# One core, gated linear attention and a tanh-shrink MLP: three sums planned apart, a load moved, a copy moved to another engine, and a new order of work

## The chip, the core and the metric

One core of one Trainium2 chip runs the whole program. The metric is device microseconds of one execution, from timed runs; beside them one execution was recorded by the profiler, and every duration below that is not a time of a run comes from that record. The engines are PE (matmuls, with weight loads shown apart as PEld), DVE and ACT (element-wise work), POOL (set-up only here) and SP (issues transfers). Each engine works through its own queue in order.

## The reference

```python
for t in range(S):                                   # q, k, v, alpha: (4, 8, 768, 48) fp32
    state = alpha[:, :, t, :, None] * state + einsum('bhd,bhe->bhde', k[:, :, t], v[:, :, t])
    y[:, :, t] = einsum('bhd,bhde->bhe', q[:, :, t], state)
x = y.transpose(0, 2, 1, 3).reshape(3072, 384)       # (B*S, H*D)
h = x @ w_in                                         # (384, 2048)
out = (h - tanh(h)) @ w_out                          # (2048, 384)
```

A recurrence over 768 tokens for 4 x 8 heads, and behind it two matrix products with h - tanh(h) between them.

## The kernel before, in words

**Units and steps.** The 3072 tokens are cut into 12 units of 256 tokens (u = 0 to 11), each of two chunks of 128 (c = 0, 1). For each unit an attention part makes `xT`, the transposed features, and an MLP part takes them through 8 steps (s = 0 to 7) of 256 hidden features each.

**The attention part.** alpha, k and q are loaded and transposed (units 0 and 1 by PE, `turn aT`, `turn kT`, `turn qT`, with alpha's results copied to SBUF by ACT and DVE, `aTa` and `aTb`; later units by DVE). DVE scans alpha's products from the end (`U`) and, scaled by the reciprocal of a chunk's whole product (`ends`), from the start (`W`); then k is multiplied by U (`kU`) and q by W (`qW`). PE transposes k back (`back`), ACT copies it (`natural`), PE forms k times v (`update`, which needs v) and the scores; DVE masks them (`masked`); PE forms the rows `y`. ACT (`x`) and DVE copy the results to `xT`; the copy named `rest` takes the last rows of 64 tokens each. For units 2 and later one PE task, the `scores` visit, forms the scores of one chunk and `y` of the chunk before in one PSUM bank pair, so the next visit waits for both copies of the one before. `moves` on SP spreads the last head pair over the tiles of `xT` by transfers, and the MLP part of the unit begins with `mix` on DVE, which reads what `moves` wrote.

**The MLP part.** Units 0 and 1 are plain matmuls (`first`, `second`). Unit 2 and later use seven products in place of eight for `second`; units 3 and later (9 units, 72 steps) do so for `first` too. In those, PE makes four products (`first_a`, L1298) in one PSUM buffer; ACT copies the first (`keep`, L1303); DVE makes three dependent sums (`partial`, L1305 to L1309): the second reads what the first wrote, the third reads both. PE makes the other products (`first`, L1314 and L1316), and DVE joins both (`join`, L1321). ACT then runs three activations (`bend`, `turn`, `square`), DVE multiplies (`shrunk`) and makes five differences (`sums`), and PE multiplies by the output weights (`second`). The buffers of `first_a` and `first` are two that rotate; `partial` frees the one, `join` the other.

**The weights** come in 16 pieces (`fetch in0` to `in7`, `out0` to `out7`) as 64-bit floats. ACT makes two passes over each (`read_a`, `read`), DVE one (`bits`) and then joins both results to the 32-bit weight (a task by the piece's own name, `in0`).

**What sets the order.** All of this is entered as tasks in a planner: a name, an engine, a planned duration, a list of tasks it comes after, and a function that emits its instructions. The order in which they are emitted, over all engines, is a written list of steps through the task list, `STEPS`; the planned durations serve in finding such a list, and in the kernel they only set how many filler matmuls (`spin`, L1479) are put into PE's planned gaps before `y 0.0`. A task that appears in one piece is emitted in one piece: `partial` is one task with three instructions, and nothing of DVE's can come between them.

**Lines the prediction touches.** `load` (L613 to L637): alpha, k, q and v of a unit in two transfers each; for unit 0 the second half is issued by ACT's queue, the first by SP's. In `go("load ...")` the list of what a load comes after. `rest` (L1040): for units 2 and later one DVE copy, L1046. `partial` (L1305). Before the change SP's queue begins: aT 0, v 0, kT 0, qT 0, fetch in0, aT 1, fetch in1, in2, in3, kT 1, qT 1, fetch out0, in4, v 1 (the names stand for loads: aT for alpha, kT for k, qT for q).

Of the kernel before, what the change touches and what calls it, by code (L numbers as in the profile page):

```python
# [17 lines left out]
P = 128  # L18
HP = 64
# [309 lines left out]
class Planner:  # L329
# [6 lines left out]
        "138 3 -2 3 -2 8 -3 17 -11 -151 143 11 -10 8 -6 12 -5 12 15 -14 -11 -8 20 -11 4 -155 163 -19 -148 149 26 -15 -2 10 -167 169 -168 160 7 -160 162 5 7 "  # L336
        "-180 160 9 -16 33 -184 2 166 -167 8 172 -178 695 -529 18 512 -694 2 -1 182 -16 3 530 -5 -527 16 4 -185 168 525 -511 -176 692 -694 167 523 -503 508 "
        "-515 511 -693 170 11 -172 689 4 -530 -171 174 524 -694 -2 182 -179 1 160 541 -535 530 -517 -178 6 690 -528 -166 2 682 11 -694 8 687 3 -522 -174 697 "
        "-693 -2 700 -525 -2 512 -509 -167 173 -181 179 516 -693 11 163 -172 2 690 -691 680 -503 -2 520 -693 2 174 -6 -166 694 -687 683 -523 -168 2 11 -9 170 "
        "-168 686 -11 -676 688 -682 685 -689 2 9 157 527 -5 -521 -166 167 -163 -2 686 -682 -1 673 11 -680 -2 6 -3 1 687 -5 -681 665 -659 676 -10 11 4 -3 4 -532 "  # L340
        "-152 685 5 -692 688 -679 -8 6 -2 -2 695 -543 521 -520 -150 671 16 -685 149 1 536 -682 687 -4 -12 -478 -46 537 4 -538 539 -541 -150 151 544 -3 -691 152 "
        "39 -37 -152 698 -547 12 -6 536 -539 4 -3 539 -17 -524 523 -512 -43 35 4 30 494 11 -526 25 505 -3 -503 -34 6 535 -527 -12 529 -522 -2 539 -531 -12 5 "
        "534 -510 9 -23 514 -521 536 -507 -2 510 -5 6 -513 -20 -4 25 513 -504 506 -33 -500 -2 30 -27 -7 30 -4 505 -500 -21 55 -36 10 501 1 -509 510 -17 -513 -4 "
        "32 26 478 -533 36 -34 32 487 -463 -60 26 35 473 -506 39 -27 -8 34 -39 510 -504 8 -12 5 24 471 9 -503 2 502 -719 720 -501 3 499 -720 252 -1 471 -484 "
        "-54 1 37 1 -222 185 529 8 -499 500 -482 1 482 -477 479 -1 -499 2 18 -6 8 -5 477 -496 25 34 -27 -27 55 -27 472 -499 -3 37 -263 735 -6 -468 26 443 -506 "
        "507 -479 474 -469 29 446 4 -735 736 1 -446 451 -483 479 -732 733 -13 6 -440 -40 -2 499 -481 475 -490 487 4 -461 462 -488 7 482 4 -17 -732 750 -486 -7 "
        "494 2 3 -4 -6 -449 -37 36 -34 501 -762 756 -751 -4 756 -18 -737 761 -10 5 6 -758 740 13 6 -758 753 7 -503 502 2 2 -488 -54 -1 40 20 11 -30 -3 -36 525 "
        "-463 480 -485 486 -480 -7 488 -480 -285 769 -489 486 -765 292 26 -28 462 -751 292 476 1 11 -10 -471 -38 510 -6 7 -488 -21 518 -484 21 -59 62 474 -533 "
        "520 -460 -26 463 24 13 -536 537 -796 292 -29 520 -11 -445 -63 62 -33 504 -796 783 -782 -10 773 20 13 -12 -492 493 12 10 -21 12 -514 537 -13 -506 497 "
        "10 -38 51 -21 -1 23 -36 23 -38 -475 476 51 -823 810 -37 38 -37 61 -834 823 -527 478 61 -24 -810 836 -552 527 24 -522 510 -11 -27 -489 503 -13 38 13 "  # L350
        "-50 1 37 2 20 -21 36 -570 556 -10 -38 49 14 -24 -38 63 -536 474 1 37 -27 63 -549 514 -840 296 531 49 -35 -840 876 -64 -811 297 -40 65 490 -514 18 497 "
        "34 -526 -10 -53 62 -5 499 34 14 -603 36 554 -535 536 -523 549 -13 -12 -534 536 -530 503 26 12 -37 -501 30 -355 827 -525 -2 576 -12 -11 -497 -355 891 "
        "-27 -37 -826 296 541 -538 576 16 -594 579 -549 567 -2 -15 -13 -507 536 -55 41 -551 511 1 -482 494 -527 39 531 10 -542 515 -25 53 -41 31 -42 54 -582 "
        "571 10 -572 20 -26 526 -523 577 -11 22 -919 879 -14 -536 591 -11 24 -35 -32 68 -13 -11 -43 1 43 24 -55 -511 -69 612 -31 32 -581 550 1 -515 554 -592 "
        "554 -883 885 50 -601 550 -883 921 -36 -551 588 13 11 -23 -37 50 -39 52 -2 -612 -4 593 -26 50 -11 -38 26 13 -38 -564 604 10 -38 39 -25 26 8 -607 3 -57 "
        "1 601 -544 604 -623 575 40 9 1 -962 300 61 577 -937 337 636 -611 600 -50 62 -632 571 -547 597 -49 61 -11 12 -975 938 26 2 -15 35 -620 610 -52 63 -627 "
        "565 52 29 -80 52 -51 52 9 1 -24 -610 584 -577 -361 989 17 -610 -41 584 12 56 -17 -50 -545 614 -1 -1007 332 658 -25 -964 939 51 28 -654 628 -15 -27 69 "
        "-11 -57 -548 575 -26 -548 549 -587 643 -44 -567 635 -13 -10 -613 -32 601 25 20 -44 -572 573 -601 667 -698 699 -661 -2 -371 978 14 -659 646 32 9 -1019 "
        "366 -33 2 73 -407 336 697 -627 -38 651 -653 654 -42 66 -23 13 -55 -642 30 678 -23 -31 44 12 -1 -22 -1 13 -666 689 -67 56 12 -23 -44 68 -67 -617 -4 665 "
        "-43 67 -66 -622 623 52 -51 -623 -3 691 -64 51 -40 54 9 -48 26 -658 -55 701 -28 63 -62 41 -714 70 604 -673 735 -61 51 11 -672 -403 1051 14 -663 685 "  # L360
        "-678 -408 1075 -51 63 -711 30 670 -51 -1024 1087 -11 -51 74 -706 684 -669 618 53 -703 675 -614 651 12 -36 37 -64 52 -51 81 -80 51 12 -11 -692 693 -697 "
        "645 -588 -79 747 -669 627 -1077 1051 51 -50 12 56 -17 -50 1 67 -1120 1121 -729 711 -12 -1090 1103 -710 738 -26 16 -689 631 14 55 -10 -58 -658 717 -58 "
        "1 58 9 -757 2 21 692 -658 4 667 -26 -642 -29 727 -760 -373 1105 -27 -700 35 721 -55 66 -769 759 -756 701 -673 739 -772 762 12 -738 737 -705 -31 726 "
        "-46 -650 -33 684 47 20 -35 -1123 1092 -684 685 66 -1158 1104 43 -735 693 54 -53 1 41 -12 24 -37 -15 41 -40 41 22 -62 51 -748 760 -62 51 13 -1 -760 698 "
        "51 -12 35 -1185 409 714 63 -62 39 12 -1174 1124 -709 710 61 -22 -751 723 -1135 1162 12 -25 26 23 -34 -735 -54 761 -760 823 -784 761 10 14 -823 36 724 "
        "-721 771 25 -779 755 -756 706 75 -74 -699 749 25 -13 -1200 1176 13 -756 -15 -417 419 781 -10 -757 -432 1175 -704 729 12 17 -28 1 -759 704 -733 31 703 "
        "1 -734 735 -714 -17 811 -42 -712 686 -716 29 688 68 -1230 1212 -49 1 -723 11 723 56 12 -809 779 -24 -13 68 -42 12 18 -1231 1244 -829 799 -38 1 55 -16 "
        "-27 -741 767 18 24 -55 32 11 -809 822 -23 24 -789 720 -745 1 745 69 -14 -29 -25 55 -44 45 -12 -32 45 -810 832 -791 781 -814 758 67 -66 45 -33 55 13 "
        "-24 -12 -771 -30 851 -13 -24 -44 -777 10 836 -68 -749 -18 -3 851 -37 -43 -767 820 28 -80 1 -768 769 51 -790 740 64 -63 -754 -54 819 -751 766 63 -858 "
        "819 -11 -27 39 -789 751 39 12 -50 40 -14 -25 12 -795 833 -810 848 -846 809 -873 874 -39 -778 -56 69 766 24 -23 -781 792 49 -35 49 -62 49 -48 1 -814 "  # L370
        "826 49 -28 -840 831 -817 841 -14 -9 10 -22 66 -43 -22 1 22 -825 814 13 10 31 -42 12 44 -877 864 -867 837 -24 55 13 -846 803 -24 -820 821 67 -34 -814 "
        "792 13 30 -20 -842 843 -23 -782 825 -893 874 -843 36 808 -12 31 12 -877 -31 878 1 -818 -27 819 -816 872 -12 -43 -816 882 -856 846 -55 -850 30 886 13 "
        "-23 -13 -32 56 13 -23 -45 -864 60 860 -43 34 -908 930 -68 -828 829 -868 898 50 -874 838 -837 805 43 26 -68 -846 889 -42 1 42 -887 3 843 42 10 14 -908 "
        "843 1 -846 911 -14 -10 11 -895 844 52 13 -12 -52 65 -54 43 20 -901 -54 907 -14 -894 922 -27 62 -9 -52 -894 956 -61 52 -883 905 -36 -26 -870 898 35 13 "
        "-12 -63 76 -926 851 76 -75 47 -894 885 -886 859 37 -36 81 -44 13 -12 -11 12 -38 -885 966 -41 10 -908 859 50 -917 879 -897 936 -13 56 -42 -920 949 -41 "
        "-27 82 -81 68 -67 81 -70 1 26 -941 950 -927 -15 25 883 35 -34 25 29 -19 -920 921 -919 895 25 18 25 -41 -1 -25 -894 962 -25 12 14 -25 1 -18 -26 1 54 14 "
        "-24 11 -950 951 -45 46 12 -57 -900 -2 903 66 -20 -14 49 -14 -974 964 -56 -911 978 -10 -45 46 -14 -31 -920 921 67 -66 -955 1022 -66 -921 922 1 1 49 "
        "-1010 3 959 -957 1020 -1024 5 1005 -23 -14 38 -970 959 12 -977 939 39 -971 993 -10 -50 40 -14 -25 -938 950 48 -10 -37 -949 997 -47 1 23 13 23 -1005 "
# [69 lines left out]
def fast(tc, q, k, v, alpha, moe_w_in, moe_w_out, out, w_in, w_out, ident, ok, pad_rows):  # L448
    nc = tc.nc
    B, H, S, D = q.shape  # L450
    NP = H // 2
# [7 lines left out]
    FS = FT // 2  # L459
# [8 lines left out]
    with ExitStack() as ctx:  # L468
# [94 lines left out]
        add = plan.add  # L563
# [1029 lines left out]
```

## Time and profile before

| what | value |
|---|---|
| timed runs | 558.57, 558.87, 559.6 us; median 558.87 |
| profiled execution | 563.36 us |
| its span, first to last instruction | 561.6 us |
| mean granted clock of PE | 0.989 |
| instructions | 15127 |
| PE in 0 to 14.0 us | 10.50 of 14.00 us busy, filler included |
| last matmul ends | near 555.6 us |
| last DVE sum ends | 556.4 us |

The profiled execution is 4.5 us longer than the median of the timed runs; 1.8 us of its time lie around its span. In groups of instructions the columns are line, engine, operation, output and inputs by tile name, shapes, count, then busy time in us, mean ns of one, and the idle time of the engine just before them with what ended it. In the timeline the columns are start, length, engine, line, operation, tiles, and in brackets idle time before. Matmuls overlap each other, so a mean of 326 ns is not the distance from one start to the next.

### The profile page before, as it was taken

To read this page: it belongs to the slowest core of one execution; us is meant where nothing else is said; L and a number is where in the kernel's file an instruction comes from. 1 tells how busy PE (TensorE), PEld (TensorE's weight loads), DVE (VectorE), ACT (ScalarE), POOL (GpSimd) and SP (SyncE) were. 2 spreads that over 40 slices of the span, in tenths; PEclk is the share of its full clock that TensorE was granted. 3 is DMA by queue.
4 is the path that set the end of the run, shared out by engine and by line. 5 is a ranking of instruction groups with operands and counts; after the bars stand their busy time and mean duration, and the time that the engine had idled before them with its cause. 6 is when DMAs were issued, how large, how long until landed. Compare 5 with 4: busy or idle time off the path is not lost. (4 is left out here: it accounts for less than half of the span.)

```text
span 561.6 us, 15127 instructions
## 1 busy us (share of the span) xinstructions
PE 547.5 (97%) x6191; PEld 501.3 (89%) x6191; DVE 484.8 (86%) x1032; ACT 393.2 (70%) x746; POOL 4.9 (1%) x23
## 2 busy tenths in 40 slices
PE   7989999999999999998999999999999999999995
PEld 6877777777999999998999999999999999999995
DVE  7578659999989899999899999999999976796773
ACT  2589898967868768978668876757955654566460
POOL 3000000000000000000000000000000000000000
PEclk9699999999999999999999999999999999999999
DMA  9988482225264473535164251123020000100001
GB/s 219 240 202 245 169 204 84 88 65 146 52 135 101 114 128 107 115 117 140 35 121 113 85 157 50 48 48 85 15 51 1 30 2 8 36 2 1 30 2 33
DMA packets 60236, 50.90 MB, mean 91 GB/s; under 512 B 35552, under 2 KB 49920, under 8 KB 60160
## 3 DMA queue, kind: packets, MB, share of 16 engines
q1 hardware_dynamic: 57536, 49.07, 34.3%
q8 instruction: 51, 0.84, 0.6%
q10 hardware_dynamic: 2624, 0.79, 0.6%
q14 instruction: 25, 0.20, 0.1%
HBM read 44.04 MB, written 4.72 MB: 87 GB/s over the span
## 5 line engine op out<-in xcount | busy, mean ns | idle before, releaser
L1383 PE MATMUL o<-b,e 128*128 128x192 f32 x480 | 94.0, 326 | 0.0
L1326 ACT ACTIVATE z<-w 128x512 f32<-128x512 f32 x72 | 45.1, 626 | 54.8 <-DVE w L1321 54.7
L1383 PEld LDWEIGHTS o<-b,e 128*128 128x128 f32 x480 | 80.1, 190 | 0.8
L1383 PE MATMUL o<-w_out,e 128*128 128x192 f32 x320 | 78.6, 327 | 0.0
L1316 PE MATMUL h<-xT,w_in 128*128 128x256 f32 x288 | 74.1, 380 | 0.0
L1383 PE MATMUL o<-b,g 128*128 128x192 f32 x320 | 69.9, 326 | 0.0
L1285 PE MATMUL h<-xT,w_in 128*128 128x256 f32 (+1 forms) x300 | 66.2, 374 | 2.0 <-DVE g L1338 1.7
L1285 PEld LDWEIGHTS h<-xT,w_in 128*128 128x128 f32 x300 | 54.4, 190 | 10.9 <-DVE g L1338 1.8
L1329 ACT ACTIVATE z<-z 128x512 f32<-128x512 f32 x96 | 60.5, 630 | 1.8
L1334 ACT ACTIVATE u<-z 128x512 f32<-128x512 f32 x96 | 60.4, 629 | 1.9
L1321 DVE TENSOR_TENSOR w<-h,u 128x512 f32<-128x512 f32 x72 | 49.0, 681 | 11.8 <-PE h L1316 11.1
L1383 PEld LDWEIGHTS o<-w_out,e 128*128 128x128 f32 x320 | 55.7, 190 | 1.5
L1298 PE MATMUL h<-xT,w_in 128*128 128x128 f32 x288 | 56.4, 278 | 0.6 <-DVE w L1321 0.5
L1298 PE MATMUL h<-xT,w_out 128*128 128x128 f32 x288 | 55.8, 275 | 0.3 <-DVE xT L1245 0.3
L1383 PEld LDWEIGHTS o<-b,g 128*128 128x128 f32 x320 | 54.1, 190 | 0.4
L1316 PEld LDWEIGHTS h<-xT,w_in 128*128 128x128 f32 x288 | 49.2, 191 | 3.7
L1338 DVE TENSOR_TENSOR g<-w,u 128x512 f32<-128x512 f32 x72 | 48.8, 680 | 3.9 <-ACT u L1334 3.6
L1343 ACT ACTIVATE big<-u 128x1024 f32<-128x1024 f32 x48 | 50.7, 1055 | 0.9
L1298 PEld LDWEIGHTS h<-xT,w_in 128*128 128x128 f32 x288 | 46.7, 191 | 2.4 <-DVE w L1321 0.8
L1350 DVE TENSOR_TENSOR e<-g 128x384 f32<-128x384 f32 x80 | 43.8, 548 | 3.8 <-PE o L1383 3.3
L1303 ACT COPY u<-h 128x128 f32<-128x128 f32 x72 | 18.8, 262 | 38.2 <-PE h L1298 32.2
L1298 PEld LDWEIGHTS h<-xT,w_out 128*128 128x128 f32 x288 | 43.7, 192 | 0.5 <-DVE xT L1245 0.5
(177 smaller groups left out, 1134.9 us busy)
## 6 DMA issues: line engine op xcount, KB each, us to landing
raw<-in_moe_w_out_dram SPq DMA_DIRECT2D x16, 768.0 KB, 4.9
raw<-in_moe_w_in_dram SPq DMA_DIRECT2D x48, 96.0 KB, 4.4
raw<-in_moe_w_in_dram SPq DMA_DIRECT2D x16, 288.0 KB, 5.2
vt<-in_v_dram SPq DMA_DIRECT2D x23, 192.0 KB, 3.9
ar<-in_alpha_dram SPq DMA_DIRECT2D x20, 192.0 KB, 3.2
kr<-in_k_dram SPq DMA_DIRECT2D x20, 192.0 KB, 3.3
qr<-in_q_dram SPq DMA_DIRECT2D x20, 192.0 KB, 3.0
raw<-in_moe_w_in_dram SPq DMA_DIRECT2D x16, 192.0 KB, 4.3
```

The costliest lines, as they stand in the source:

```text
L1285: T.matmul(h[:, a, to], lhsT=w_in[:, j, f * P:(f + 1) * P], rhs=xT[u][:, j, to], start=(j == 0), stop=(j == KT - 1))
L1298: T.matmul(h[:, i], lhsT=left[n][:, s], rhs=right[u][n], start=i == 0, stop=True, skip_group_check=True)
L1303: A.copy(m["kept", s][:, 0], m["part", s][:, 0])
L1316: T.matmul(h[:, 2 * a:2 * a + 2].rearrange("p i t -> p (i t)"), lhsT=wi[:, KT - 1, s, a], rhs=xT[u][:, KT - 1, :], start=False, stop=True, ...
L1321: V.tensor_add(m["w", s], m["h", s].rearrange("p i t -> p (i t)"), m["u", s])
L1326: A.activation(m["z", s], m["h", s], AF.Tanh, scale=TA / W_SCALE)
L1329: A.activation(m["z", s], m["z", s], AF.Arctan, scale=TB)
L1334: A.activation(m["u", s], m["z", s], AF.Square, scale=TK * W_SCALE ** -0.5)
L1338: V.tensor_mul(g.rearrange("p a c t -> p (a c t)"), m["h", s], m["u", s])
L1343: A.activation(big, m["us", s // 2].rearrange("p s t -> p (s t)"), AF.Relu, bias=-F_FAST, scale=W_SCALE, accum_out=over[:, n:n + 1])
L1350: V.tensor_sub(e[:, 0:3, :], x[:, 3:4].to_broadcast([P, 3, P]), x[:, 0:3])
L1383: T.matmul(o[n][:, i], lhsT=g_, rhs=w_, start=(s_ == 0 and (n, i) in ((0, 0), (1, 0), (2, 1), (3, 0))), stop=(s_ == FS - 1), skip_group_ch ...
```

## The change

Three edits to the tasks, one to planned durations, and a new list of steps.

1. `partial` becomes three tasks, `partial_a`, `partial_b` and `partial`, with one sum each. Each comes after the one before; `join` and the PSUM buffer wait for the last, as before.
2. `load v 0` comes after `load kT 0` and `load qT 0`; a weight fetch that comes first in the list has `load aT 1` ahead of it.
3. From unit 4 on, the copy `rest` is ACT's (16 tasks).
4. Planned durations of the weight pieces, of `keep`, `join` and `rest` are changed.

```diff
-            add(f"fetch {what}{s}", "SP", ..., [held and f"read {held[0]}{held[1]}", held and f"bits {held[0]}{held[1]}"],
+            add(f"fetch {what}{s}", "SP", ..., [held and f"read {held[0]}{held[1]}", held and f"bits {held[0]}{held[1]}", n == 0 and "load aT 1"],
...
-            add(f"read_a {what}{s}", "ACT", 1.05, rank, there, lambda do=do: do(0))
-            add(f"read {what}{s}", "ACT", 1.05, rank, [f"read_a {what}{s}"], lambda do=do: do(1))
-            add(f"bits {what}{s}", "DVE", 0.6, rank, there, lambda do=do: do(2))
-            add(f"{what}{s}", "DVE", 1.0, rank, [f"read {what}{s}", f"bits {what}{s}"], lambda do=do: do(3))
+            add(f"read_a {what}{s}", "ACT", 0.96, rank, there, lambda do=do: do(0))
+            add(f"read {what}{s}", "ACT", 0.96, rank, [f"read_a {what}{s}"], lambda do=do: do(1))
+            add(f"bits {what}{s}", "DVE", 0.5, rank, there, lambda do=do: do(2))
+            add(f"{what}{s}", "DVE", 0.9, rank, [f"read {what}{s}", f"bits {what}{s}"], lambda do=do: do(3))
...
-                   + [u == 1 and ("kUb 0" if what == 3 else "turn qT 0")]
+                   + [u == 1 and ("kUb 0" if what == 3 else "turn qT 0")] + [u == 0 and what == 3 and x for x in ("load kT 0", "load qT 0")]
...
-                        V.tensor_copy(to, m["y", c].rearrange("p r g t -> p r (g t)")[0:ROWS, :, NP * (HP + D):])
+                        (A.copy if u >= 4 else V.tensor_copy)(to, m["y", c].rearrange("p r g t -> p r (g t)")[0:ROWS, :, NP * (HP + D):])
...
-                    go_c("rest", "DVE", 0.26, 10.5, [y, f"first {u - 2}:{FS - 1}"], rest)
+                    go_c("rest", "ACT" if u >= 4 else "DVE", 0.27, 10.5, [y, f"first {u - 2}:{FS - 1}"], rest)
...
-                def partial():
+                def partial(n):
                     kept, part = m["kept", s], m["part", s]
-                    V.tensor_add(kept[:, 1], kept[:, 0], part[:, 1])
-                    V.tensor_add(kept[:, 2], kept[:, 1], part[:, 2])
-                    V.tensor_add(kept[:, 1::2], kept[:, 1:3], part[:, 3:4].to_broadcast([P, 2, P]))
+                    if n < 2:
+                        V.tensor_add(kept[:, n + 1], kept[:, n], part[:, n + 1])
+                    else:
+                        V.tensor_add(kept[:, 1::2], kept[:, 1:3], part[:, 3:4].to_broadcast([P, 2, P]))
...
-                    add(f"keep {me}", "ACT", 0.26, r + 0.1, [f"first_a {me}"] + old_u, keep)
-                    add(f"partial {me}", "DVE", 0.75, r + 0.2, [f"keep {me}"], partial)
+                    add(f"keep {me}", "ACT", 0.2, r + 0.1, [f"first_a {me}"] + old_u, keep)
+                    add(f"partial_a {me}", "DVE", 0.2, r + 0.2, [f"keep {me}"], lambda: partial(0))
+                    add(f"partial_b {me}", "DVE", 0.2, r + 0.21, [f"partial_a {me}"], lambda: partial(1))
+                    add(f"partial {me}", "DVE", 0.34, r + 0.22, [f"partial_b {me}"], lambda: partial(2))
```

The list of steps is wholly new, with 2116 tasks where there were 1972. Read out by names, the queues begin as follows.

| queue | before | after |
|---|---|---|
| SP | aT 0, v 0, kT 0, qT 0, in0, aT 1, in1, in2, in3, kT 1, qT 1, out0, in4, v 1 | qT 0, aT 0, kT 0, kT 1, qT 1, aT 1, v 0, in0, in1, in2, in3, v 1, out0, in4 |
| PE | turn aT 0, turn kT 0, turn qT 0, back 0.0, update 0.0, scores 0.0, back 0.1, scores 0.1, y 0.0, turn aT 1, carried 0.1, y 0.1, first_a 0:0, first 0:0, update 0.1, first 0:1, turn kT 1, turn qT 1, first 0:2, back 1, first 0:3 | turn qT 0, turn aT 0, turn kT 0, back 0.0, update 0.0, scores 0.0, back 0.1, turn aT 1, scores 0.1, turn qT 1, carried 0.1, y 0.0, y 0.1, first_a 0:0, update 0.1, first 0:0, turn kT 1, first 0:1, back 1, first 0:2, scores 1.0, first 0:3 |
| DVE | aTb 0, Ua 0, Ub 0, endsa 0, kUa 0, Wa 0, endsb 0, qWa 0, Wb 0, kUb 0, qWb 0, masked 0.0, decay 0.1, bits in0, masked 0.1, in0 | aTb 0, Ub 0, Ua 0, kUa 0, least 0, kUb 0, endsa 0, endsb 0, Wa 0, qWa 0, Wb 0, qWb 0, masked 0.0, decay 0.1, aTb 1, bits in0, U_b 1, masked 0.1, U 1, ends 1, in0, W_a 1, least 1, bits in1, W 1, state 0.1, bits in2, in1, decay 1.0, kUa 1, qWa 1, kUb 1, shrunk 0:0, in2 |

PE's queue holds 527 tasks in both. DVE's has 870 in place of 742 (144 more by the parted sums, 16 fewer by the copies), ACT's 627 in place of 611, SP's 92 in both. The end of the order is the same in both: `second 11:6`, `gather`, `second 11:7`, `ok`, `see` and the last sums and stores.

## The prediction

> **What bounds the kernel now.** I read the page's busy times and slices first, then busy time by stage in windows of 14 us and of 1 us, then the timeline of the start, then the groups of instructions. The page:
>
> ```profile
> PE 547.5 (97%) x6191; PEld 501.3 (89%) x6191; DVE 484.8 (86%) x1032; ACT 393.2 (70%) x746; POOL 4.9 (1%) x23
> ...
> PE   7989999999999999998999999999999999999995
> ...
> DVE  7578659999989899999899999999999976796773
> ...
> PEclk9699999999999999999999999999999999999999
> ```
>
> PE is busy 547.5 of 561.6 us, and its work is the same before and after, so only its idle time, its filler matmuls and the stretch at a lower clock (second slice, 6 tenths) can be won. The last slice is half empty: closing sums and output transfers behind the last matmul, which the new order leaves in place. The middle, by windows:
>
> ```profile
> 252.70:266.80 14.10, 12.36 (x183) 11.56 (x182) 13.59 (x28) 11.60 (x23) 0.00 (x0) 1.00 0.58 142
> 266.80:280.80 14.00, 13.54 (x209) 12.62 (x208) 12.54 (x27) 9.27 (x20) 0.00 (x0) 1.00 0.11 34
> ```
>
> Columns: stretch, length, busy us of PE, weight loads, DVE, ACT, POOL, clock, DMA share, GB/s. These two lose 1.74 and 0.46 us of PE. With 0.32, 0.07 and 0.03 in the three windows from 196.6 to 238.7, the middle loses 2.6 us in all. In the worst window DVE is busy 13.59 of 14.10: where PE waits there, DVE is full. The start, in windows of 1 us:
>
> ```profile
> 11.00:12.00 1.00, 0.85 (x9) 0.60 (x7) 0.97 (x5) 0.49 (x1) 0.00 (x0) 1.00 1.12 174
> 12.00:13.00 1.00, 0.00 (x0) 0.00 (x0) 1.00 (x2) 0.00 (x0) 0.00 (x0) 1.00 1.21 284
> 13.00:14.00 1.00, 0.23 (x5) 0.23 (x7) 1.00 (x3) 0.00 (x0) 0.00 (x0) 0.80 1.01 271
> 14.00:15.00 1.00, 1.00 (x17) 0.91 (x17) 0.59 (x1) 0.30 (x2) 0.00 (x0) 0.50 1.09 231
> ...
> 23.00:24.00 1.00, 1.00 (x46) 1.00 (x48) 0.00 (x0) 0.92 (x2) 0.00 (x0) 0.58 1.09 194
> 24.00:25.00 1.00, 1.00 (x52) 0.83 (x43) 0.43 (x1) 1.00 (x2) 0.00 (x0) 1.00 1.25 189
> ```
>
> PE stands still for two microseconds, then runs at half clock from about 13.8 to 24.0. The timeline gives the places:
>
> ```profile
> 11.54 0.32 PE L1088 MATMUL y<-vt,kn 128*64 128x48 f32 x3
> 13.77 0.88 PE L1088 MATMUL y<-vt,kn 128*48 128x48 f32 x13 [1.92 <-issue]
> ...
> 27.20 2.94 PE L1285 MATMUL h<-xT,w_in 128*128 128x128 f32 x24
> ...
> 37.23 2.86 PE L1285 MATMUL h<-xT,w_in 128*128 128x256 f32 x12 [1.68 <-DVE g L1338]
> ```
>
> The stop splits the matmuls of `update 0.0` after the third of 16, and no semaphore ends it ("issue"). The other mark to keep is 37.23, the start of `first 0:2`.
>
> **What the Trainium skill says.** "TensorE: Matmul & The Clock Gate", What's actually happening: the array falls to half rate after an idle window of some 3.4 us and is released after a busy one; windows run freely. The trace agrees in kind: half rate for 10.24 us, behind a window that held the 1.92 us stop; release took three such lengths, not one. "Runtime: NRT & Kernel Launch", Instruction fetch mechanics: instructions come in 16 KiB blocks by the sequencer's own DMA queue, mostly hidden. The page has such a queue (51 packets, 0.84 MB, 16 KiB each); that this fetch is the 1.92 us stop is my inference, and then it was not hidden. "DMA: Bandwidth & Descriptors", Issuing engines are not separate DMA queues: SP's and ACT's transfers share 16 engines. The trace agrees: the DMA share is 1.0 and more at 11 to 15 us, so an earlier place for one load is a later one for another.
>
> **The change, part by part.** The groups that price it:
>
> ```profile
> L1307 DVE TENSOR_TENSOR u<-u,h 128x128 f32<-128x128 f32 x72 | 20.0, 278 | 9.5 <-ACT u L1303 9.3
> L1308 DVE TENSOR_TENSOR u<-u,h 128x128 f32<-128x128 f32 x72 | 20.7, 287 | 2.5
> L1309 DVE TENSOR_TENSOR u<-u,h 128x256 f32<-128x256 f32 x72 | 30.3, 421 | 2.5
> ...
> L1046 DVE COPY xT<-sc 112x128 f32<-112x128 f32 x20 | 5.5, 274 | 1.3 <-PE h L1016 1.1
> ...
> L1065 ACT COPY xT<-h 112x128 f32<-112x128 f32 x20 | 5.4, 269 | 0.0
> ```
>
> (1) *Three sums apart.* No instruction is added. DVE stood idle 2.5 us ahead of the second sums and 2.5 ahead of the third; other work can now lie there: at best 5.0 us of DVE in 366 us where it is full. The price: a sum that is interleaved holds its PSUM buffer longer, and `first_a` of a later step waits for it. One foreign instruction is 0.42 to 0.68 us, and PE has other matmuls queued, so 0 to 3 us in all; I take 0.4.
>
> (2) *Last rows on ACT from unit 4.* 16 copies: DVE loses 16 x 0.274 = 4.4 us, ACT gains 16 x 0.27 = 4.3. ACT is 70% busy; behind each copy waits the next activation, 0.27 us late. Waiting for the rows are the next visit of scores and products, which needs the bank, and `moves` on SP. The sum reading the moved rows waited 1.4 us in 2 places in all, so a later `moves` costs at most tenths. On the path: 0 (bounds -0.5 and +1.5; if ACT's cover goes, 16 x 0.27 = 4.3).
>
> (1) and (2) give DVE up to 9.4 us, but PE lost only 2.6 in the middle. I take 2.3 of it back (bounds 2.6 back, or 2 more lost, as an order has its own rough places).
>
> (3) *Start reordered.* SP now issues q, a, k of unit 0, then k, q, a of unit 1, then half of v, then w_in. (a) Alpha is one load later. A load of 384 KB at the 304 GB/s of the windows 4 to 8 us is 1.26 us; the issue in front is some 0.5 us. PE's `turn qT` takes the slow slot (the first turn took 2.27 us, later ones 1.1), and `turn aT` ends near 4.1 + 2.27 + 1.15 = 7.5. DVE begins at 7.5 instead of 6.43. (b) DVE's chain to `qWb`, by the timeline's durations: copy 0.69, two scans 2.35, kUa 0.66, least 0.16, kUb 0.66, ends 0.26 + 0.27, scan 1.22, qWa 0.66, scan 1.22, qWb 0.68 = 8.83, so 16.3; qWa is done at 14.4. (c) v's SP half is behind 7 loads' worth of bytes, 2.75 MB: at 304 GB/s from 2.0 us it lands at 11.0, by the rates that the windows really had at 12.9. `update 0.0` wants it at 12.0 (kUa 10.5, `back`, copy by ACT), and PE's next task, `scores 0.0`, is not ready before 14.4. So v is hidden by 1.5 us. (d) DVE onward: masked 1.29, decay 0.35, copy 0.69, bits 0.55, scan 1.23, masked 1.29, scan 1.23, ends 0.37, in0 0.96 = 7.96: `first_a 0:0` at 24.3 (before 27.20). Then 1.22 + 0.16 + 0.55 + 1.22 + 0.35 + 0.55 + 0.96 = 5.01: `first 0:1` at 29.3. Then 0.35 + 3 x 0.67 + 0.68 + 0.96 = 4.0: `first 0:2` at 33.3, with `back 1` (0.93) already done. Before: 37.23, and 0.37 idle at 41.22. Gain 3.9 + 0.93 + 0.37 = 5.2. w_in's first piece, behind 3.54 MB at 265 GB/s, lands at 15.4 and is wanted by ACT at 18.5: hidden. This holds at full clock: filler matmuls are set into the planned gaps, and the block of instructions that was late is asked for during `turn aT`, near 6.8, and needed near 12.
>
> Sum on the profiled execution: -5.2 - 2.3 + 0.4 = -7.1, from 563.36 to **556.3**. The median of the timed runs, 558.87, is 4.5 below the profiled one, about what a stop of 1.9 us and ten microseconds at half clock cost. I hold it likeliest that the timed runs did not have that stretch; then of the 7.1 only 2.6 is left to win, from 558.87: again 556.3. Which it is, no row tells; 0.2% (1.1 us) is about what a measurement of this kernel can tell from no change.
>
> **Rivals.** *The timed runs had the half clock too.* For it: they lie within 1 us, as one state would. Against it: the 4.5 us. Then all 7.1 count: 551.8. *Slower: v comes late.* DMA rates of 174 to 206 GB/s at 9 to 12 us speak for it, the 304 of the small-row loads against. PE stands at `update 0.0` with `scores 0.0` queued behind it. Once v lands after 14.4 every microsecond counts one for one; from about 1.9 us of standing still within one clock window, the half clock returns. 4.5 for that, less the 2.3 of the middle, plus 0.4: 561.5 against the median. *Nothing won.* The order was already at PE's floor, its start's gain is none without the half clock, and the 2.6 us of stalls come back in other places: 558.9. For it: PE full in nearly every window.
>
> **Chances.** Forecast 0.45, half clock in the timed runs 0.22, late v 0.15, nothing won 0.18. Faster by over 0.2%: 0.38 of the forecast's 0.45, all 0.22, 0.08 of the last: 0.68. Within: 0.05 + 0.08 = 0.13. Slower: 0.02 + 0.15 + 0.02 = 0.19. Range 551.0 to 560.5: it takes in the second case's value and the forecast's bounds (2 us more lost in the middle, 3 for held buffers), and leaves out most of the late-v case and the tail of the first rival.
>
> **What would show it.** Right: no half clock after 7 us, `first 0:2` near 33.3, under 1 us of PE idle from 196 to 281, no gaps left ahead of the second and third sums. Wrong: PE idle ahead of L1088 with v as the releaser; a half clock elsewhere; new PE waits for the sums of L1307 to L1309 or for ACT's copies.

## The result and the profile after

Median of 13 timed runs 557.27 us (556.26 to 558.95), against 559.23 us (557.84 to 562.42) for 13 of the kernel before: ratio 0.9959, 95% interval 0.9940 to 0.9979. The forecast was 556.3 us, 0.9954 of the median known then. The profiled execution took 558.13 us with a span of 556.3, where that of before took 563.36 and 561.6. Some executions of this program have a stretch of some ten microseconds in which PE is granted half its clock, and the profiled one of before was such an execution (mean clock 0.989; runs without the stretch show 0.995 to 1.0).

The page after, same lines as shown of before:

```profile
PE 544.8 (98%) x6191; PEld 498.5 (90%) x6191; DVE 478.1 (86%) x1016; ACT 398.2 (72%) x762; POOL 4.9 (1%) x23
...
PE   8989999999999999999999999999999999999996
...
DVE  6977469999999899999999999999999976667863
...
PEclk9999999999999999999999999999999999999998
```

The second slice is at full clock. The start in windows of 1 us (PE, weight loads, DVE, ACT, POOL, clock, DMA share, GB/s):

```profile
11.00:12.00 1.00, 0.82 (x6) 0.46 (x5) 1.00 (x3) 1.00 (x2) 0.00 (x0) 1.00 0.94 214
12.00:13.00 1.00, 1.00 (x6) 0.57 (x5) 0.93 (x6) 0.78 (x4) 0.00 (x0) 1.00 0.93 249
13.00:14.00 1.00, 1.00 (x14) 0.83 (x14) 1.00 (x1) 0.07 (x1) 0.00 (x0) 1.00 0.89 238
14.00:15.00 1.00, 0.68 (x18) 0.56 (x16) 0.96 (x3) 0.32 (x1) 0.00 (x0) 1.00 0.94 221
```

No microsecond is empty, and the clock column stays at 1.00. The timeline of PE at the marks of the prediction:

```profile
13.80 0.67 PE L1091 MATMUL y<-vt,kn 128*64 128x48 f32 x16
24.77 0.60 PE L1288 MATMUL h<-xT,w_in 128*128 128x128 f32 x3
25.68 1.16 PE L1288 MATMUL h<-xT,w_in 128*128 128x128 f32 x9 [0.31 <-issue]
...
30.54 2.86 PE L1288 MATMUL h<-xT,w_in 128*128 128x256 f32 x12 [0.48 <-DVE w_in L99]
...
39.61 2.83 PE L1288 MATMUL h<-xT,w_in 128*128 128x256 f32 x12 [1.24 <-DVE g L1342]
```

`update 0.0` runs in one piece of 16 and waits for no v. `first_a 0:0` begins at 24.77 (forecast 24.3), `first 0:1` at 30.54 (29.3), `first 0:2` at 34.45 (33.3; 37.23 in the profiled execution of before). A stop without a semaphore is still there, but it is now short and inside `first_a 0:0`; the last line is a wait that the prediction did not have, `first 0:3` for the DVE product that frees its buffer.

The sums taken apart, as groups:

```profile
L1311 DVE TENSOR_TENSOR u<-u,h 128x128 f32<-128x128 f32 x144 | 38.4, 280 | 11.7 <-ACT u L1306 10.5
L1313 DVE TENSOR_TENSOR u<-u,h 128x256 f32<-128x256 f32 x72 | 29.2, 414 | 0.9
```

First and second sums share a line of the kernel now. Idle time ahead of the third fell from 2.5 to 0.9 us; for the first two together it is 1.2 us beside the waits for ACT, where it was 2.5 ahead of the second alone. From 196.6 to 280.8 us, where the prediction asked for less than 1 us of idle PE, it is 0.98, against 2.61 before.

**Two marks that can be compared.** When PE begins `first 1:0`, and again when it begins `first_a 3:0`, its queue has done exactly the same tasks in both orders. So these starts, and the time from the second to the start of the last output product, measure two stages. Each value is of one profiled execution; 5.0 to 6.7 us follow the last product.

| kernel | first 1:0 | first_a 3:0 | from there to the last product |
|---|---|---|---|
| before, with the half-clock stretch | 71.92 | 167.48 | 387.81 |
| before, run again, without it | 67.00 | 162.56 | 387.44 |
| after | 69.35 | 164.91 | 385.73 |

At full clock the new start is 2.35 us longer, and what follows is 1.7 shorter in this pair. One execution of each is little to go by: the same order of the rest takes 387.4 to 389.2 us in the traces below.

### The profile page after: what moved, and what is told of

Read it like the earlier page. It is cut to its first block, busy times and chain, and to the rows that moved or that the text cites. A ratio compares the mean times of both kernels' runs of the same rounds, so it can differ in the third digit from the quotient of the medians.

```text
span 556.3 us, 15117 instructions
## 1 busy us (share of the span) xinstructions
PE 544.8 (98%) x6191; PEld 498.5 (90%) x6191; DVE 478.1 (86%) x1016; ACT 398.2 (72%) x762; POOL 4.9 (1%) x23
## 5 line engine op out<-in xcount | busy, mean ns | idle before, releaser
L1311 DVE TENSOR_TENSOR u<-u,h 128x128 f32<-128x128 f32 x144 | 38.4, 280 | 11.7 <-ACT u L1306 10.5
```

The source lines that it names most:

```text
L1311: V.tensor_add(kept[:, n + 1], kept[:, n], part[:, n + 1])
```

## Experiments

Theory A, from the prediction: the half-clock stretch belongs to the profiled execution of before and few others; the gain in the median comes from the middle, through DVE. Rival B: the stretch is in the timed runs, and the start makes the gain. Rival C: in the middle it is the new order as such and not the parted sums. Theory F: the stop in `update 0.0` is a block of PE's instructions that arrives late. The transfer meant is the first that PE's instruction queue (51 transfers of 16 KB) shows in the span; the trace does not number the blocks.

**The kernel before again**, unchanged.

> The kernel before, unchanged, for the granted clock of its timed runs. Theory A (the half-clock stretch at 14 to 24 us belongs to the profiled execution and a few timed runs; the median gain of the change comes from the middle): mean clock 0.997 or more in most timed runs, 558 to 560 us, and the few at 561 to 563 us have about 0.989. Rival B (the stretch is in the timed runs too; the gain is the start's): mean clock about 0.989 in most.

Measured: 558.51 us, ratio 0.9987 (0.9960 to 1.0013), which is what the same kernel shows against itself. Of its 22 runs 5 have a mean clock of 0.989 to 0.992 and a median of 562.63 us; the other 17 show 0.996 or more and 558.14. Of the 75 runs of before beside it 18 had the stretch (563.09 against 558.58). So neither a lone accident nor the rule: about one run in five, 4.5 us each. Its profiled execution has the stop without the half clock:

```profile
11.30 0.32 PE L1088 MATMUL y<-vt,kn 128*64 128x48 f32 x3
13.24 0.55 PE L1088 MATMUL y<-vt,kn 128*48 128x48 f32 x13 [1.63 <-issue]
```

The same place, 1.63 us in place of 1.92, and the clock stays full; the two executions are 4.9 us apart at both marks above. This pair does not show that the length of the stop decides. Stops of 1.68 us (in before, ahead of `first 0:2`), of 1.74 (below) and even one of 2.35 (in joined_plain) were followed by full clock. The half-clock stretches last 10.24 us in the first profiled execution of before and 6.83 in fewer_fillers, three and two times 3.41, so the clock seems to change in steps of 3.41 us; where a stop falls in these steps may count as well, and no run here varies it.

The timeline also gives the two marks of the prediction for before at full clock:

```profile
22.15 2.94 PE L1285 MATMUL h<-xT,w_in 128*128 128x128 f32 x24
...
32.17 2.86 PE L1285 MATMUL h<-xT,w_in 128*128 128x256 f32 x12 [1.67 <-DVE g L1338]
```

Here `first_a 0:0` begins at 22.15 and `first 0:2` at 32.17, before the forecast of 24.3 and 33.3 for the changed kernel.

**The start of one, the rest of the other.** The two lists are cut at `first 0:7`, some 62 us in.

```diff
-order = changed
+cut = changed.index("first 0:7")
+order = sorted(changed[:cut], key=before.index) + changed[cut:]
```

> The changed kernel with the tasks of the start (all that its list has ahead of first 0:7, some 62 us) in the order that they have in the kernel before. A: the start is about neutral at full clock, so the ratio to before stays near 0.996 (0.994 to 0.998); where a profile or run falls to half clock at 14 us it is some 4 us longer. B: the gain is gone, 0.999 to 1.001.

Measured: 557.09 us, 0.9970 (0.9951 to 0.9989), against 558.99 of before beside it. Five of 22 runs had a mean clock of 0.988 to 0.992 (559.65), the other 17 a median of 556.93, 1.65 us less than the 558.58 of before. The gain stays without the new start: B falls. The cut itself costs 1.5 us here: PE waits once, at 66.20, for an output weight that the mixed list brings late.

```diff
-order = before
+cut = before.index("first 0:7")
+order = sorted(before[:cut], key=changed.index) + before[cut:]
```

> The kernel before with the tasks of its start (all ahead of first 0:7) in the order that they have in the changed kernel; the rest as before. A: about as before, 0.998 to 1.001 by the median, but without the slow runs at 561 to 563 us. B: 0.992 to 0.997, no half clock at 14 us.

Measured: 560.37 us, 1.0025 (1.0010 to 1.0040), no half clock in 22 runs. The new start alone makes the kernel slower: 1.8 us more than the full-clock runs of before beside it (558.58). It was expected neutral. Part of this is seen at its very beginning: with alpha loaded second, DVE starts on it at 7.19 us here and at 7.71 in the changed kernel, against 6.19 in before run again.

**The sums together again**, in the changed order, first at the place of the last, then at the place of the first.

```diff
-partial_a ... partial_b ... partial
+... partial_a partial_b partial
```

> The changed kernel with the three dependent sums next to each other again, at the place of the last; all else in the changed order. If taking the sums apart is what relieves the middle (A): idle time of 2 to 5 us ahead of the second and third sums comes back, PE loses 1 to 2.5 us more in the middle, ratio to before 0.998 to 1.000. If the new order by itself makes the gain (rival C): 0.995 to 0.997, as the change.

Measured: 559.08 us, 0.9997 (0.9978 to 1.0016). The gain over before is gone. Only the first and second sums move in this edit (128 tasks; the other 16 already stood next to the third). But beside it new_start, with nearly the same start and the old rest, took 560.37: 1.3 us of the new rest's advantage are still there with the sums together.

```diff
-partial_a ... partial_b ... partial
+partial_a partial_b partial ...
```

> The changed kernel with the three sums next to each other at the place of the first in place of the last. If what counts is the idle time between dependent sums (2.5 us ahead of the second and of the third) and the room for other work between them, it loses as the other one did: PE 2 to 3 us idle in 168 to 450 us, ratio 0.998 to 1.001. If sums_together lost because the first sums came late, this one keeps the gain: 0.995 to 0.997.

Measured: 558.90 us, 0.9976 (0.9961 to 0.9992), between what the two readings foretold. Half-clock runs in its before (8 of 56) flatter it: against the 559.48 of those without, it gains 0.6 us, where rows_on_dve below, with the same start and the sums apart, gains 1.6 in the same way of counting. Busy times in 168.5 to 450 us, one line for each kernel, in the order before again, after, sums together, sums early:

```profile
168.50:450.00 281.50, 279.09 (x3206) 268.46 (x3205) 271.80 (x606) 208.79 (x418) 0.00 (x0) 1.00 0.32 81
```

```profile
168.50:450.00 281.50, 280.27 (x3219) 270.13 (x3218) 267.02 (x596) 211.44 (x429) 0.00 (x0) 1.00 0.32 82
```

```profile
168.50:450.00 281.50, 278.80 (x3201) 267.30 (x3200) 271.17 (x594) 208.81 (x427) 0.00 (x0) 1.00 0.32 82
```

```profile
168.50:450.00 281.50, 279.65 (x3208) 268.70 (x3207) 272.21 (x596) 209.25 (x427) 0.00 (x0) 1.00 0.32 82
```

DVE (third number) is busy 267.0 us with the sums apart and 271.2 and 272.2 with them together. These windows do not hold quite the same work; over the whole executions, with the same 1016 instructions, it is 478.1 apart, and 485.4 and 485.3 together. The sums themselves take only 3.3 and 3.5 us of this (67.6 us apart, 70.9 and 71.1 together). The rest is overlap, as two stretches of DVE's timeline show, first before run again, then after:

```profile
264.44 0.29 DVE L1307 TENSOR_TENSOR u<-u,h 128x128 f32<-128x128 f32 x1
264.76 0.29 DVE L1308 TENSOR_TENSOR u<-u,h 128x128 f32<-128x128 f32 x1
265.08 0.42 DVE L1309 TENSOR_TENSOR u<-u,h 128x256 f32<-128x256 f32 x1
265.42 0.69 DVE L1338 TENSOR_TENSOR g<-w,u 128x512 f32<-128x512 f32 x1
```

```profile
261.23 0.28 DVE L1311 TENSOR_TENSOR u<-u,h 128x128 f32<-128x128 f32 x1
261.43 0.68 DVE L1342 TENSOR_TENSOR g<-w,u 128x512 f32<-128x512 f32 x1
262.03 0.28 DVE L1311 TENSOR_TENSOR u<-u,h 128x128 f32<-128x128 f32 x1
262.34 0.42 DVE L1313 TENSOR_TENSOR u<-u,h 128x256 f32<-128x256 f32 x1
```

A sum that needs the one just before it starts 0.03 us after that one's end (264.73 to 264.76); an operation that does not need it starts 0.08 us before the end (265.42 against 265.50, 261.43 against 261.51). By these lines each pair of dependent sums in a row costs DVE about 0.11 us (an estimate from these starts), of which the idle time that the prediction read shows only 0.03.

PE is idle 1.2 us in the windows above with the sums apart, 2.7 and 1.9 with them together, 2.4 before. Both ways of taking them together lose, so it is not only the lateness of the first two sums. Against before at full clock the two kernels stand at +0.5 and -0.6 us, and rows_on_dve, which has them apart, at -1.6: parting them is worth 1.0 to 2.1 us by the timed runs. C does not fall altogether: the new start alone stands at +1.8, so 1.3 to 2.4 us more come from the new order behind its start (the copies, tried below, show no gain). The traces show little of that share (388.3 and 387.0 us from `first_a 3:0` on, against 387.6 in new_start); what makes it stays open.

**Where DVE's lateness reaches PE**, in the kernel before run again:

```profile
259.63 0.68 DVE L1321 TENSOR_TENSOR w<-h,u 128x512 f32<-128x512 f32 x1
260.22 1.22 DVE L815 TENSOR_TENSOR_SCAN W<-aT,before 128x516 f32<-128x516 f32 x1
260.34 0.63 ACT L1326 ACTIVATE z<-w 128x512 f32<-128x512 f32 x1 [0.81 <-DVE w L1321]
260.36 0.30 PEld L1314 LDWEIGHTS h<-xT,w_in 128*128 128x128 f32 x2 [2.14 <-DVE w L1321]
```

The join that frees PE's buffer ends at 260.31, and PE's weight load starts 0.05 us later, after 2.14 us without one; PE itself stood idle for 1.74 us. DVE had not idled before it.

**The copies on DVE again.**

```diff
-(A.copy if u >= 4 else V.tensor_copy)(to, ...)
+V.tensor_copy(to, ...)
...
-go_c("rest", "ACT" if u >= 4 else "DVE", 0.27, ...
+go_c("rest", "DVE", 0.27, ...
```

> The changed kernel with the copies of the last rows on DVE again for all units, at the same place in the order. By the prediction's term (4.4 us of DVE, little of it on the path): 0 to 1.5 us longer than the change, 0.996 to 0.999 of before. If the copies are what relieves the middle (rival to the sums): 2 us longer, 0.999 or more. If ACT's copies delay the visits: shorter than the change, under 0.995.

Measured: 556.70 us in 10 runs, 0.9964 (0.9947 to 0.9981). That is about the change's own ratio (0.9959), with intervals of some 0.2% on each: moving the copies won nothing that can be seen. Its profiled execution even has PE busy 281.46 of 281.50 us in the stretch above.

**The load of v alone.** One line moves in the order of before.

```diff
 load aT 0
-load v 0
 load kT 0
 load qT 0
+load v 0
 fetch in0
```

> The kernel before with one edit of its order: the load of v of unit 0 is issued behind k and q. v lands some 1.3 us later and is still hidden: ratio 0.999 to 1.001, the stop in update 0.0 at the same matmul, and half-clock runs in a like share (10 to 35%). If v's place is what makes the stop or the slow start, the stop is longer or gone and the share changes.

Measured: 558.67 us in 18 runs, 0.9972 (0.9958 to 0.9985), and not one run with the half clock, where 8 of the 56 of before beside it had it. If nothing had changed, none in 18 would still come up about once in sixteen times (48/56 to the 18th power), so the count alone is not strong. The timeline says more:

```profile
4.00 3.52 PE L749 MATMUL turned<-ident,rough 64*64 64x64 f32 x125
...
7.38 1.13 PE L749 MATMUL sc<-ident,rough 64*64 64x64 f32 x63
8.45 1.98 PE L1479 MATMUL spin<-after,ident 128*128 128x512 f32 x4
...
11.44 0.99 PE L1088 MATMUL y<-vt,kn 128*64 128x48 f32 x16
```

With k and q earlier, PE turns alpha, k and q without a pause (before, `turn kT` began at 8.23), has gone through more instructions by 7 us, and the transfer of its next block begins at 9.32 in place of 10.4 to 10.9. All 16 matmuls of `update 0.0` follow within 0.99 us. A rest of the stop is left: the 7th begins at 11.65 and the 8th at 11.99, with PE idle for 0.12 us. In before, too, PE stops when it has made 223 weight loads, but there this is behind the 3rd matmul (v_behind has four fillers fewer ahead). Its start is 67.20 at the first mark, against 67.00 for before at full clock. Against the full-clock runs of before (559.48) the edit gains 0.8 us.

**Fewer fillers**, for F.

```diff
+fillers = [n for n, x in enumerate(filled) if x[1] == -1]
-return filled
+return [x for n, x in enumerate(filled) if n not in fillers[:5]]
```

> The kernel before without its first five filler matmuls (ten rows of the trace, some 20 instructions with their weight loads). If the stop inside update 0.0 is the arrival of PE's third block of instructions (theory F), it stays at the same count of instructions and so moves ten matmuls on: behind the 13th of the 16 of update 0.0 in place of the 3rd. If it is the arrival of v or anything tied to a task (rival), it stays behind the 3rd.

```profile
12.52 0.55 PE L1089 MATMUL y<-vt,kn 128*64 128x48 f32 x12
15.05 0.29 PE L1089 MATMUL y<-vt,kn 128*64 128x48 f32 x4 [1.98 <-issue]
```

The stop moved from behind the 3rd to behind the 12th, where F said 13th. In before and here it lies between PE's 223rd and 224th weight load: the count of instructions fits, the task does not. One execution, 562.03 us, with 6.83 us at half clock.

**More instructions early.** Thirty small matmuls take the place of the five fillers ahead of the first turn.

```diff
-filled += [(free, -1, do, None)] * int(...)
+filled += [(free, -1, small if first else do, None)] * int(...)
...
+for _ in range(6):
+    T.matmul(spun[0][0:HP, 0:HP], lhsT=ident[0:HP, 0:HP], rhs=ident[0:HP, 0:HP], start=True, stop=True)
```

> The kernel before with its first five fillers (128x128) replaced by thirty matmuls of 64x64 in the same gap, so that PE has gone through some 100 instructions more when the first turn begins. F: the block is asked for earlier (its transfer starts near 8.5 us in place of 10.4 to 10.9) and the stop of 1.2 to 1.9 us in update 0.0 is under 0.7 or gone; no timed run of some 22 falls to a mean clock of 0.992 or less (of before's 75, 18 did); median 557.3 to 558.3, ratio 0.995 to 0.999. Rival: stop and slow runs stay, ratio 1.000.

Measured: 563.54 us in 6 runs, 1.0084 (1.0064 to 1.0104). The stop is gone (`update 0.0` runs 0.67 us in one piece, no run of 6 at half clock), but not in the way that F foretold: the transfer begins at 10.76, no earlier than in before. The 60 rows of fillers took 6.55 us and held the first turn up to 7.8 us, so that PE comes to its 224th weight load only at 13.7, 1.5 us after the transfer's end (12.19). My size for the fillers was wrong by four microseconds, and the expected time missed.

**Old start and new rest, without the cut's wait.** After 462 tasks the two lists have done the same set; they can be joined there.

```diff
-order = changed
+order = before[:462] + changed[462:]
```

> The first 462 tasks in the order of the kernel before (the two lists agree there as sets), the rest in the order of the changed kernel, with all its edits, and the thirty small fillers. A and F together: the old start at full clock (2.2 us better than the changed start by the traces at 62 us) and the new middle (2 to 3 us better than the old): 554 to 555.5 us, 0.991 to 0.994 of before, and better than the change. If the start's order made the change's gain (B): 0.998 or more.

With the small fillers in it, 558.81 us, 0.9999 (0.9982 to 1.0017), spoilt by the same 3 to 4 us at the start and by a stop of 1.62 us at 50.5 (first_a 3:0 at 167.66); from there it needs 383.68 us. That stop, too, ends 1.4 us after a block's transfer (50.73 to 52.11), so the fillers had moved the trouble on. One of its 22 runs, 563.13 us, has a mean clock of 0.993.

> The first 462 tasks in the order of the kernel before, the rest in the order of the changed kernel, with all its edits and the fillers of the kernel before. A: the old start with its share of runs at half clock (about one in four or five, 4 to 5 us longer), and the new middle: at full clock 554.5 to 556 us, ratio to before 0.991 to 0.995. If the old order of start and the new middle do not add up, 0.996 or more.

Without them: 559.19 us, 0.9977 (0.9961 to 0.9993); 8 of 22 runs with a mean clock of 0.988 to 0.994 (559.96), the other 14 at 558.08. Missed by 2 us. Its profiled execution has a stop of 2.35 us without a semaphore at 206.68, behind a visit's burst of small matmuls; the block of instructions ended its transfer at 205.14. The clock stays full behind it.

> The same with the first five fillers replaced by thirty matmuls of 64x64 that go round four quarters of the array, like those of the turns ([...]some 2.1 us in all; thirty on one quarter took 6.5 us). F: [...]the block's transfer starts near 8.3, the stop falls into turn qT near 10 us and is at most 1 us; no run at half clock from 14 us on; 554 to 555.5 us, 0.990 to 0.994, and a narrower spread than joined_plain. Rival: the stop keeps its length and the share of half-clock runs stays.

```diff
-    T.matmul(spun[0][0:HP, 0:HP], lhsT=ident[0:HP, 0:HP], rhs=ident[0:HP, 0:HP], start=True, stop=True)
+    x, to = halves[n // 2 % 2], halves[n % 2]
+    T.matmul(spun[n // 2 % 2][to, 0:HP], lhsT=ident[x, x], rhs=ident[x, x], start=True, stop=True)
```

Going round four quarters of the array, the same 60 rows took 2.40 us. The block's transfer begins at 8.01, near the 8.3 that was expected, and `update 0.0` runs in one piece; but PE stops for 1.15 us at 47.81, behind as many weight loads (859) as in joined. Measured: 556.93 us in 7 runs, 0.9956 (0.9931 to 0.9980), none at half clock. The time is 1.4 us above what was expected: the fillers delay `turn kT` to 9.48. It is no better than the change by any margin that this shows; no version here beats both kernels clearly.

**All stages in one table** (profiled executions, one of each):

| kernel | start and rest | first_a 3:0 | from there to the last product |
|---|---|---|---|
| before again | old, old | 162.56 | 387.44 |
| v alone | old with v moved, old | 162.76 | 389.18 |
| new_start | new, old | 163.91 | 387.62 |
| after | new, new | 164.91 | 385.73 |
| old_start | old, new | 164.44 | 384.50 |
| joined_quad | old, new | 164.50 | 383.98 |
| joined_plain | old, new | 162.79 | 387.69 (with the 2.35 us stop) |
| rows_on_dve | new, new | 164.81 | 384.01 |
| sums_together | new, new but sums together | 163.75 | 388.33 |
| sums_early | new, new but sums together | 164.32 | 386.97 |
| fewer_fillers | old with fewer fillers, old | 167.09 | 388.23 |
| early_fillers | old with small fillers, old | 165.72 | 388.49 |
| joined | old with small fillers, new | 167.66 | 383.68 |

With the old rest 387.4 to 389.2 us; with the new one 383.7 to 385.7, and 387.7 once; with the sums together 387.0 and 388.3.

Timed runs tell only their mean clock, not where it fell. A mean of 0.994 or less was seen in 35 of 184 runs of before, 13 of 44 of old_start and joined_plain, 1 of 22 of joined, none of 13 of early_fillers and joined_quad, none of 89 with the new start and none of 18 with v moved. In before such runs were 4.5 us longer, in old_start and joined_plain only 2.7 and 1.9; why they lose less is not shown.

## Why the prediction was right, and where not

The number was right, but by luck: two terms were wrong, in opposite directions, and nearly cancelled. The forecast for the median was a gain of 2.6 us, 0.7 from the start and 1.9 from the rest. The timed runs show a start that loses 1.8 us and a rest that wins about 3.4.

**The half clock and the median.** I held it likeliest that the timed runs did not have the stretch. Four in five do not, one in five does. Its loss is worth 4.5 us where it occurs in before, and 0.4 us of the median (558.99 of all runs against 558.58 of those without). What the prediction gave as the reason fits the runs: in the changed kernel the block's transfer begins at 8.55 us in place of 10.4 to 10.9, PE comes to its 224th weight load only at 13.8, and no stop is left there. v's edit by itself brings the transfer forward, too. What began as an inference is now better supported: the stop stays at the 223rd weight load when the tasks around it move, and PE resumes 1.3 to 1.6 us after the end of the transfer in every such stop (12.23 to 13.77 in before; 205.14 to 206.68 in joined_plain). That the fetch is the cause is argued from count and time; no record says so.

**The start at full clock: the step that failed.** Of 5.2 us of gain I gave 4.5 to the half clock, which leaves 0.7 of gain at full clock. Measured: a loss of 1.8 us (new_start against before's full-clock runs), 2.35 at first_a 3:0. The chain through DVE was right within about 1.2 us: turn aT near 7.5 (7.65), first_a 24.3 (24.77), first 0:1 29.3 (30.54), first 0:2 33.3 (34.45). What I did not do was to work out the same chain for before without its stop. There `first 0:2` begins at 32.17, so that even the 33.3 of the forecast was a loss of 1.1 us, and `first 1:0` at 67.00. I compared with a disturbed execution and subtracted a round figure, although the prediction itself has DVE begin later (7.5 in place of 6.43). And I followed the chain only to first 0:2; the wait of 1.24 us at 39.61 lies behind it.

**The middle: undersized.** Forecast -2.3 + 0.4 = -1.9; this pair of traces shows -1.7, the other kernels with the new rest up to -3.8, one +0.25. The timed runs give about -3.4 (the change's -2.0, less 0.4 for the half clock, set against new_start's +1.8). Right in sign and in place. The cause named, the sums taken apart, is shown for 1.0 to 2.1 us of it, and DVE is relieved by more than the 5.0 us of idle time that the prediction counted, since dependent sums in a row also lose the overlap with their neighbours. The remainder belongs to the new order by itself or to something that was not tried alone. Buffers held longer cost nothing that shows.

**The copies.** Forecast 0 on the path: no run contradicts it, within about 1 us.

**v late.** It landed in time; that rival fell. v's edit, the one part of the start that was tried alone, gained 0.8 us at full clock; if the parts add up, the loss of the new start comes from its other parts.

**The account.** Start at full clock +1.8 to +2.35, rest -1.7 to -3.8, half clock gone from the median -0.4: between -2.4 and +0.25, measured -2.0 (559.23 to 557.27). So wide a sum confirms no single term.

## What to carry to other kernels

Before costing a change against a trace, ask whether the trace is a typical run: a mean clock of 0.989 and 4.5 us above the median said that it was not, and every term at that place should then have been worked out twice, with the disturbance and without. Where an engine is nearly full, dependent small operations in a row can cost more than their durations and the idle time between them: look also for the overlap that they lose. Letting the planner place them one by one was the largest part of the gain that could be tied to one edit here. When a forecast comes out right, check its terms one by one; here two errors cancelled. And a queue that starts with bursts of tiny instructions may run into the arrival of its own next block: here the stop shrank when the early matmuls followed each other without a pause (v's load alone), and stayed when filler was taken away (one execution).

## What was not expected of the hardware

With the old start PE went through 223 weight loads and as many matmuls and stopped for 1.2 to 2.0 us with nothing to wait for that the profile shows (0.12 us with v moved). Each stop ended 1.3 to 1.5 us after a 16 KB transfer of PE's instruction queue.

A stop of 2.35 us and several of 1.63 to 1.74 left the clock at full rate; 1.92 and 1.98 were followed by half rate, for 10.24 us in before and 6.83 in fewer_fillers. So the idle window of some 3.4 us with which the prediction worked is longer than the stops that were enough here, and the length of a stop does not settle it.

On DVE an operation that does not need the one before it started 0.08 us before that one's end, a dependent one 0.03 us behind it. Sixty 64x64 matmuls to one quarter of the array took 6.55 us, over four quarters 2.40 us.
